# Requests on Pool spread out, and weight differences on VectorE placed behind PSUM copies, in an attention and maxout kernel

## The chip, the cores and the metric

The kernel runs on one core of a Trainium2 chip. The metric is the device time of one execution in microseconds. A core has five engines that matter here, each with its own instruction stream that it runs in order: PE (matrix multiply), DVE (VectorE), ACT (ScalarE), POOL (GpSimd, called Pool in the text) and SP (which only issues transfers). An engine that waits at one instruction runs nothing behind it.

## The reference, cut to what matters

Causal attention in blocks of 64 over 8 batches of 8 heads (576 positions, head size 64), and a maxout layer on its result:

```
scores = (q @ k^T) / 8, masked by blocks of 64;  a = softmax(scores);  x = a @ v
x      -> [4608 tokens, 512]
g      = maximum(x @ w1, x @ w2)            # 512 -> 1024
out    = g @ w_out                          # 1024 -> 512
```

The kernel rewrites the maxout. With D = w1 - w2, maximum(x w1, x w2) = x w2 + relu(x D). So

```
out = x @ M + relu(x @ D) @ w_out,   M = w2 @ w_out  (512 x 512, worked out once)
```

D is made by VectorE in four quarters of 256 columns, each as soon as that quarter of w1 has landed. M is made by TensorE in eight units: unit (i, c) is half i of the columns and row block c, and needs half i of w_out.

## The kernel before: the parts that matter

The program is a list of instructions that the author has put in order by hand (`manual_schedule`). The order of the calls below is, for each engine, the order in which that engine runs its share.

Loading and preparing. A "group" g is four heads, and has a request for q and one for k, 576 KB each. A request on SP is tied to Pool: a one-column memset of the target is put on Pool, and SP's request has to follow it. Requests of w1, w_out, w2 and v are issued by Pool itself.

```python
raw  = tile_pool(bufs=3)      wraw = tile_pool(bufs=4)
ps_s = PSUM pool, bufs=2 (scores)      ps_m = PSUM pool, bufs=4 (all else)

def load_qk(g, queues, gated=False):
    for nm, src, queue in (("q", q, queues[0]), ("k", k, queues[1])):
        if queue is None ...: continue
        raws[nm, g] = t = raw.tile([P, 2, RPP * D], FP32)
        if gated:
            nc.gpsimd.memset(t[:, 0, :1], 0.0)               # L114, Pool
        queue.dma_start(out=t[:], in_=...)                   # L115, SP

def cast(nm, g, parts):                  # fp32 -> bf16, on the engine that is named
    for copy, j0, j1 in parts:
        copy(out=n[:, j0:j1], in_=t[:, j0:j1])               # L155

def load_w1(j):                          # quarter j of w1, 512 KB
    nc.gpsimd.dma_start(out=w1_raw[j], in_=w1r[...])         # L177, Pool
def diff_w(j):                           # D of quarter j
    nc.vector.tensor_sub(d_sb[quarter j], w1_raw[j], w2_sb[j])   # L183, VectorE
def load_wo(i):                          # half i of w_out
    nc.gpsimd.dma_start(out=wo_sb[half i], in_=wor[...])     # L189, Pool
```

The units of TensorE that are put in wherever there is room. `fill(n)` emits the next ones: 8 matmuls of an M unit count 4, the 4 matmuls of an h unit count 4.

```python
def h_unit(i, f):      # 512 tokens i, 128 columns f of D; f = 2j, 2j+1 need diff_w(j)
    pt = ps_m.tile(...)
    for c in range(4):
        matmul(pt, d_sb[:, c, f], xT[:, c, tokens])          # L226
    nc.vector.tensor_scalar_max(g[:, f], pt, 0.0)            # L231, the relu

def m_unit(i, c):
    pt = ps_m.tile(...)
    for f in range(8):
        matmul(pt, bT_sb[:, f, c], wo_sb[:, f, half i])      # L249
    (act if i and c > 1 else dve)(out=m_sb[:, c, half i], in_=pt)    # L254

def transposes(nm, g, copies):           # two ps_m tiles; returns their copy-out
    for j in range(9):
        for i in range(2): nc.tensor.transpose(pts[i][:, j], n[...], ident)  # L357
    # copy_out: copies[i](out=qT or kT, in_=pts[i])                          # L365
```

The stage that is changed, as it was (cuts marked by dots):

```python
    av(2, [0, 1]); burst_q3(2); masks_q(2)
    load_qk(2, (SP, SP), gated=True)
    ...                                       # fills, bursts of scores, av
    burst_q3(3); masks_q(3)
    load_w1(0)
    load_qk(3, (SP, None), gated=True)        # q of group 3
    cast("q", 2, ((pool, 0, RPP),))
    load_qk(3, (None, SP), gated=True)        # k of group 3
    for j in range(1, d_ff // WB): load_w1(j)
    load_v(1, 0); load_v(1, 1)
    fill(8)                                   # M 0, 1
    av(3, [2, 3, 4])
    fill(4)                                   # M 2
    x_out(1, 0, NCH, (act, act))
    cast("k", 2, ((act, 0, RPP),))
    fill(4)                                   # M 3
    diff_w(0)
    fill(8)                                   # M 4, 5
    transposes("q", 2, (dve, act))()
    fill(4)                                   # M 6
    transposes("k", 2, (act, act))()
    pad_keys(4); pad_keys(5)
    diff_w(1)
    cast("q", 3, ((pool, 0, RPP),))
    load_v(1, 2); load_v(1, 3)
    load_qk(4, (SP, SP), gated=True)
    cast("k", 3, ((pool, 0, RPP),))
    load_v(1, 4)
    fill(4)                                   # M 7
    region(tile_0(4), tile_1(4), masked=False)
    fill(8)                                   # h 0, 1
    diff_w(2)
    region(tile_2(4), tile_0(5), masked=False)
    masks(4)
    fill(8)                                   # h 2, 3
    diff_w(3)
    copy_out = transposes("q", 3, (dve, act)) # ... h 4, transposes of k 3, and the main loop
```

Of the kernel before, what the change touches and what calls it, by code (L numbers as in the profile page):

```python
# [14 lines left out]
def kernel(  # L15
# [10 lines left out]
    nc = tc.nc  # L26
# [6 lines left out]
    d_model = H * D  # L33
    d_ff = moe_w1.shape[1]
    NDM = d_model // P
    NFF = d_ff // P
# [7 lines left out]
    RPP = S // NP  # L44
# [9 lines left out]
    NCH = 5  # L54
# [44 lines left out]
    wo_sb = wpool.tile([P, NFF, d_model], BF16, name="wo_sb")  # L99
# [5 lines left out]
    dve, pool, act = nc.vector.tensor_copy, nc.gpsimd.tensor_copy, nc.scalar.copy  # L105

    def load_qk(g, queues, gated=False):
        b, u = divmod(g, GPB)
        for nm, src, queue in (("q", q, queues[0]), ("k", k, queues[1])):
            if queue is None or by_dma(nm, g):  # L110
                continue
            raws[nm, g] = t = raw.tile([P, 2, RPP * D], FP32, name=f"{nm}raw")
            if gated:
                nc.gpsimd.memset(t[:, 0, :1], 0.0)  # L114
            queue.dma_start(  # L115
                out=t[:],
                in_=src[b, 4 * u:4 * u + 4].rearrange(
                    "(s h) (p t) d -> (h p) s (t d)", h=2, t=RPP),
            )
# [4 lines left out]
    def by_dma(nm, g):  # L124
        return g >= T_DMA.get(nm, NG)
# [21 lines left out]
    def cast(nm, g, parts):  # L147
        if by_dma(nm, g):
            return
        t = raws[nm, g].rearrange("p s (t d) -> p t s d", d=D)  # L150
        if (nm, g) not in qk_n:
            qk_n[nm, g] = qkn.tile([P, RPP, 2, D], BF16, name=f"{nm}n")
        n = qk_n[nm, g]
        for copy, j0, j1 in parts:
            copy(out=n[:, j0:j1], in_=t[:, j0:j1])  # L155
# [12 lines left out]
    WB = 256  # L168
# [6 lines left out]
    def load_w1(j):  # L175
        w1_raw[j] = wraw.tile([P, NDM, WB], FP32, name="w1raw")
        nc.gpsimd.dma_start(out=w1_raw[j][:], in_=w1r[:, :, j * WB:(j + 1) * WB])  # L177
# [4 lines left out]
    def diff_w(j):  # L182
        nc.vector.tensor_sub(d_sb[:, :, j * WB:(j + 1) * WB], w1_raw[j][:], w2_sb[j])  # L183
# [8 lines left out]
    dve, pool, act = nc.vector.tensor_copy, nc.gpsimd.tensor_copy, nc.scalar.copy  # L192
    SP, ACT = nc.sync, nc.scalar
    warm = small.tile([P, 1], FP32, name="warm")
# [132 lines left out]
    def fill(n):  # L327
        while n > 0:
            if not current:
                k = next((k for k, t in enumerate(todo) if t[2] <= done_tokens[0]), None)  # L330
                if k is None:
                    return max(0, n)
                current.append(todo.pop(k))
            t = current[0]
            next(t[1])
            n -= t[3]
            t[0] -= 1
            if not t[0]:
                current.pop()
        return 0  # L340
# [10 lines left out]
    def transposes(nm, g, copies):  # L351
        n = qk_n.pop((nm, g))
        pts = [ps_m.tile([P, RPP, NP], BF16, name=f"ps_{nm}T", tag="m") for _ in range(2)]
        for j in range(RPP):
            for i in range(2):
                r = slice(i * NP, (i + 1) * NP)
                nc.tensor.transpose(  # L357
                    pts[i][:, j, :], n[r, j].rearrange("p s d -> p (s d)"), ident[r, r],
                )

        def copy_out(which=(0, 1), part=(0, NP), copy=None):
            p0, p1 = part
            for i in which:
                t = (qT_r if nm == "q" else kT_r)[(2 * g + i) % NT]
                (copy or copies[i])(  # L365
                    out=t[:, p0 * RPP:p1 * RPP].rearrange("q (p j) -> q p j", j=RPP),
                    in_=pts[i][:, :, p0:p1].rearrange("q j p -> q p j"),
                )
        return copy_out

    def scores(p, ps, col, c, q0, w):
        qT, kT = qT_r[p % NT], kT_r[p % NT]
        k0 = min(c * P, S - P)
        for hh in range(2):
            r = slice(hh * D, (hh + 1) * D)
            nc.tensor.matmul(  # L376
                ps[:, hh, col:col + w], kT[r, k0:k0 + P], qT[r, q0:q0 + w],
                start=True, stop=True,
            )
# [9 lines left out]
    def corner_scores(p, ps, col):  # L389
        qT, kz = qT_r[p % NT], kz_r[p % NT]  # L390
        for k0, q0 in ((0, 384), (BLK, 512)):
            for hh in range(2):
                r = slice(hh * D, (hh + 1) * D)
                nc.tensor.matmul(  # L394
                    ps[:, hh, col:col + BLK], kz[r, k0:k0 + P], qT[r, q0:q0 + BLK],
                    start=(k0 == 0), stop=(k0 > 0),
                )

    def exp(p, ps, w, a0):
        nc.scalar.activation(  # L400
            out=aT_r[p % NA][:, :, a0:a0 + w], in_=ps[:, :, :w], func=AF.Exp, scale=scale,
        )

    def mask(p, a0, eng=None):
        (eng or nc.gpsimd).memset(aT_r[p % NA][BLK:, :, a0:a0 + BLK], 0.0)  # L405
# [20 lines left out]
    def burst_q3(p, warm=0):  # L426
        burst(p, ((3, 384, 192),), 1408, warm)
# [5 lines left out]
    def masks_q(p, eng=None):  # L433
        for a in (1024, 1408):
            mask(p, a, eng)
# [3 lines left out]
    def tile_0(p):  # L439
        u = ps_s.tile([P, 2, 512], FP32, name="ps_s", tag="s")  # L440
        scores(p, u, 0, 0, 0, 512)
        return lambda masked: (exp(p, u, 512, 0), masked and mask(p, 0))
# [7 lines left out]
    def tile_2(p):  # L450
        u = ps_s.tile([P, 2, 512], FP32, name="ps_s", tag="s")
        corner_scores(p, u, 320)
        scores(p, u, 0, 2, 256, 320)
        scores(p, u, 384, 3, 448, P)

        def out(masked):
            exp(p, u, 512, 1024)
            nc.scalar.activation(
                out=aT_r[p % NA][BLK:, :, 1536:AW], in_=u[BLK:, :, 320:320 + BLK],
                func=AF.Exp, scale=scale,  # L460
            )
            if masked:
                mask(p, 1024)
                mask(p, 1344)
        return out

    def masks(p):
        for a0 in (0, 576, 1024, 1344):
            mask(p, a0)

    def region(*tiles, masked=True):
        for out in tiles:
            out(masked)
# [29 lines left out]
    def x_by_dma(g):  # L503
        return BY_DMA <= g < NG - 1
# [10 lines left out]
    def x_out(g, t0=0, t1=NCH, copies=(dve, dve)):  # L515
        b, u = divmod(g, GPB)
        if x_by_dma(g):
            if u == GPB - 1:
                done_tokens[0] = (b + 1) * S
            return  # L520
        xp = xps[g]
        n = t1 - t0
        n_odd = min(t1, NCH - 1) - t0
        pe = ps_m.tile([P, 2, n, BLK], BF16, name="ps_xe", tag="m")
        po = ps_m.tile([P, 2, n_odd, BLK], BF16, name="ps_xo", tag="m")
        for s in range(2):
            for t in range(t0, t1):
                src = xp[:, s, t].rearrange("p a d -> p (a d)")
                nc.tensor.transpose(pe[:, s, t - t0, :], src[:BLK], ident[:BLK, :BLK])
                if t < NCH - 1:  # L530
                    nc.tensor.transpose(po[:, s, t - t0, :], src[BLK:], ident[BLK:, BLK:])
        dst = xT[:, 2 * u:2 * u + 2, b * S + t0 * P:b * S + t1 * P].rearrange(
            "p s (t h w) -> p s t h w", h=2, w=BLK)
        copies[0](out=dst[:, :, :, 0], in_=pe[:])
        copies[1](out=dst[:, :, :n_odd, 1], in_=po[:])
        if u == GPB - 1:
            done_tokens[0] = min(b * S + t1 * P, (b + 1) * S)
# [91 lines left out]
    av(2, [0, 1])  # L629
    burst_q3(2)  # L630
    masks_q(2)
    load_qk(2, (SP, SP), gated=True)
    fill(2)
    burst_q1(3)
    fill(2)
# [2 lines left out]
    av(2, [2, 3, 4])  # L638
    burst_q3(3)
    masks_q(3)  # L640
    load_w1(0)
    load_qk(3, (SP, None), gated=True)
    cast("q", 2, ((pool, 0, RPP),))
    load_qk(3, (None, SP), gated=True)
    for j in range(1, d_ff // WB):
        load_w1(j)
    load_v(1, 0)
    load_v(1, 1)
    fill(8)
    av(3, [2, 3, 4])  # L650
    fill(4)
    x_out(1, 0, NCH, (act, act))
    cast("k", 2, ((act, 0, RPP),))
    fill(4)
    diff_w(0)
    fill(8)
    transposes("q", 2, (dve, act))()
    fill(4)
    transposes("k", 2, (act, act))()
    pad_keys(4)  # L660
    pad_keys(5)
    diff_w(1)
    cast("q", 3, ((pool, 0, RPP),))
    load_v(1, 2)
    load_v(1, 3)
# [2 lines left out]
    load_v(1, 4)  # L668
    fill(4)
    region(tile_0(4), tile_1(4), masked=False)  # L670
    fill(8)
    diff_w(2)
    region(tile_2(4), tile_0(5), masked=False)
    masks(4)
    fill(8)
    diff_w(3)
    copy_out = transposes("q", 3, (dve, act))
    outs = tile_1(5), tile_2(5)
    copy_out()
# [96 lines left out]
```

## Time and profile before

| | before |
|---|---|
| median of 3 runs | 258.56 us (258.22 to 259.25) |
| span of the profiled execution | 256.4 us |
| PE busy | 241.1 us (94%) |
| DVE busy | 150.6 us (59%) |
| ACT busy | 120.6 us (47%) |
| POOL busy | 121.0 us (47%) |
| granted TensorE clock | 0.998 |

The page gives busy times over the whole span. A view of windows gives, for each stretch of time, the busy microseconds of each engine with the number of instructions in brackets. A timeline gives start, duration, engine and source line of each instruction, and in square brackets how long the engine had been idle before it and who released it. The list of waits adds these idle times up by pair, as total, count and longest. The chain is followed back from the last instruction, at each step to what released it. A transfer's time "to landing" runs from the start of its issue.

### The profile page before, as it was taken

To read this page: it belongs to the slowest core of one execution; us is meant where nothing else is said; L and a number is where in the kernel's file an instruction comes from. 1 tells how busy PE (TensorE), PEld (TensorE's weight loads), DVE (VectorE), ACT (ScalarE), POOL (GpSimd) and SP (SyncE) were. 2 spreads that over 40 slices of the span, in tenths; PEclk is the share of its full clock that TensorE was granted. 3 is DMA by queue.
4 is the path that set the end of the run, shared out by engine and by line. 5 is a ranking of instruction groups with operands and counts; after the bars stand their busy time and mean duration, and the time that the engine had idled before them with its cause. 6 is when DMAs were issued, how large, how long until landed. Compare 5 with 4: busy or idle time off the path is not lost.

```text
span 256.4 us, 6716 instructions
## 1 busy us (share of the span) xinstructions
PE 241.1 (94%) x2732; PEld 133.2 (52%) x2768; DVE 150.6 (59%) x301; ACT 120.6 (47%) x159; POOL 121.0 (47%) x288
## 2 busy tenths in 40 slices
PE   8798887998999999999999999999999999999994
PEld 2466743565555555555555555455545564444443
DVE  4987469657485457545753575357635754753521
ACT  2876378657774655646464646464646300000000
POOL 1972673669769466955675577547231100000000
PEclk9999999999999999999999999999999999999999
DMA  7999999779999999999999999999961312111122
GB/s 243 216 159 226 348 326 205 221 60 217 158 177 190 163 239 153 233 166 223 145 209 161 220 146 205 158 218 166 108 139 58 81 43 82 42 42 42 73 90 83
DMA packets 104383, 41.27 MB, mean 161 GB/s; under 512 B 89248, under 2 KB 93728, under 8 KB 104352
## 3 DMA queue, kind: packets, MB, share of 16 engines
q0 software_dynamic: 65952, 11.87, 60.4%
q1 hardware_dynamic: 37984, 28.32, 48.7%
q10 hardware_dynamic: 416, 0.66, 0.7%
q8 instruction: 21, 0.34, 0.6%
q14 instruction: 10, 0.08, 0.1%
HBM read 34.60 MB, written 9.44 MB: 172 GB/s over the span
## 4 chain that ended last, share of the span: by engine, by line
PE 85%; DMA 5%; DVE 4%; issue 3%; ACT 2%; POOL 0%; POOLq 0%
PE ps_y L268 35%; PE ps_h L226 23%; PE ps_o L491 11%; PE ps_s L376 8%; DMA w1raw<-in_moe_w_dram 3%; DMA qraw<-in_q_dram 2%; PE ps_w L346 2%; PE ps_qT L357 2%; DVE d_sb L183 2%; ACT aT L400 2%; DVE g L231 1%; PE ps_y L283 1%; PE ps_s L394 1%; PE ps_s L411 1%; PE ps_bT L238 0%
## 5 line engine op out<-in xcount | busy, mean ns | idle before, releaser
L400 ACT ACTIVATE aT<-ps_s 128x1024 bf16<-128x1024 f32 (+2 forms) x100 | 95.8, 994 | 45.4 <-PE ps_s L376 33.9
L226 PE MATMUL ps_h<-xT,d_sb 128*128 128x512 bf16 x277 | 67.1, 379 | 2.7 <-DVE qT L365 1.0
L268 PE MATMUL ps_y<-wo_sb,g 128*128 128x512 bf16 x261 | 66.7, 379 | 2.6 <-issue 2.5
L231 DVE TENSOR_SCALAR g<-ps_h 128x512 bf16<-128x512 f32 x72 | 49.4, 689 | 16.4 <-PE ps_h L226 16.4
L405 POOL MEMSET aT<- 64x128 bf16 x128 | 22.8, 200 | 65.6 <-ACT aT L400 64.7
L273 DVE COPY y<-ps_y 128x512 f32<-128x512 f32 x35 | 24.2, 691 | 46.2 <-PE ps_y L268 45.6
L491 PEld LDWEIGHTS <-aT 128*128 128x128 bf16 x960 | 37.4, 98 | 14.0 <-issue 0.7
L226 PEld LDWEIGHTS <-d_sb 128*128 128x128 bf16 x288 | 26.5, 98 | 32.8 <-issue 4.1
L268 PEld LDWEIGHTS <-g 128*128 128x128 bf16 x280 | 24.8, 98 | 30.2 <-issue 5.5
L491 PE MATMUL ps_o<-vv,aT 128*128 128x65 bf16 x960 | 39.8, 194 | 0.0
L268 PE MATMUL ps_y<-m_sb,xT 128*128 128x512 bf16 x136 | 37.2, 379 | 0.4 <-issue 0.2
L159 POOL DMA_DIRECT2D vv<-in_v_dram x40 | 34.1, 859 | 0.9 <-issue 0.5
L376 PE MATMUL ps_s<-qT,kT 64*128 64x128 bf16 (+6 forms) x344 | 31.4, 281 | 1.6 <-ACT kT L365 0.7
L498 DVE TENSOR_TENSOR xp<-ps_o,rec 128x256 bf16<-128x256 f32 (+1 forms) x64 | 31.4, 491 | 2.2
L132 POOL DMA_DIRECT2D kb<-in_k_dram x40 | 29.4, 761 | 0.0
L497 DVE RECIPROCAL rec<-ps_o 128x4 f32<-128x4 f32 (+1 forms) x64 | 12.0, 187 | 24.1 <-PE ps_o L491 23.4
L288 ACT COPY y<-ps_y 128x256 f32<-128x256 f32 (+1 forms) x2 | 0.6, 319 | 49.3 <-PE ps_y L283 49.3
L365 ACT COPY qT<-ps_qT 128x576 bf16<-128x576 bf16 x15 | 9.6, 639 | 23.3 <-PE ps_qT L357 21.8
L155 POOL CAST qn<-qraw 128x1152 bf16<-128x1152 f32 (+1 forms) x15 | 16.5, 1100 | 7.6 <-DMA qraw<-in_q_dram 7.6
L268 PEld LDWEIGHTS <-xT 128*128 128x128 bf16 x140 | 12.8, 98 | 14.0 <-issue 0.7
L376 PEld LDWEIGHTS <-kT 64*128 64x128 bf16 x344 | 11.8, 94 | 12.4 <-issue 7.1
L365 DVE COPY qT<-ps_qT 128x576 bf16<-128x576 bf16 x17 | 12.7, 749 | 0.5 <-PE ps_qT L357 0.5
(58 smaller groups left out, 137.3 us busy)
## 6 DMA issues: line engine op xcount, KB each, us to landing
qraw<-in_q_dram SPq DMA_DIRECT2D x16, 576.0 KB, 5.0
out_dram<-y SPq DMA_DIRECT2D x35, 256.0 KB, 4.1
vv<-in_v_dram POOLq DMA_DIRECT2D x32, 128.0 KB, 5.8
kraw<-in_k_dram SPq DMA_DIRECT2D x5, 576.0 KB, 7.6
kb<-in_k_dram POOLq DMA_DIRECT2D x40, 72.0 KB, 6.8
w1raw<-in_moe_w_dram POOLq DMA_DIRECT2D x4, 512.0 KB, 7.1
xT<-in_moe_w_dram POOLq DMA_DIRECT2D x4, 256.0 KB, 6.5
wo_sb<-in_moe_w_out_dram POOLq DMA_DIRECT2D x2, 512.0 KB, 10.3
```

Of the source, the lines that this page charges most:

```text
L132: nc.gpsimd.dma_start(out=n[h * BLK:(h + 1) * BLK, :, s], in_=(q if nm == "q" else k)[b, 4 * u + 2 * s + h].rearrange("(j p) d -> p j d", ...
L159: nc.gpsimd.dma_start(out=vv_r[b % NV][P - rows:, c, :, :D], in_=v[b, :, c * P:c * P + rows, :].rearrange("h p d -> p h d"),)
L226: nc.tensor.matmul(pt[:], d_sb[:, c, f * P:(f + 1) * P], xT[:, c, t0:t0 + SPAN], start=(c == 0), stop=(c == NDM - 1),)
L231: nc.vector.tensor_scalar_max(g[:, f], pt[:], 0.0)
L268: nc.tensor.matmul(py[:], lhs, rhs, start=(n == 0), stop=(n == len(terms) - 1),)
L273: nc.vector.tensor_copy(out=y[:], in_=py[:])
L365: (copy or copies[i])(out=t[:, p0 * RPP:p1 * RPP].rearrange("q (p j) -> q p j", j=RPP), in_=pts[i][:, :, p0:p1].rearrange("q j p -> q p j"),)
L376: nc.tensor.matmul(ps[:, hh, col:col + w], kT[r, k0:k0 + P], qT[r, q0:q0 + w], start=True, stop=True,)
L400: nc.scalar.activation(out=aT_r[p % NA][:, :, a0:a0 + w], in_=ps[:, :, :w], func=AF.Exp, scale=scale,)
L405: (eng or nc.gpsimd).memset(aT_r[p % NA][BLK:, :, a0:a0 + BLK], 0.0)
L491: nc.tensor.matmul(po[:, gi, hh, :], a[:, hh, a0:a0 + P], vv[:, c, h0 + 2 * hh, :], start=(mm == 0), stop=(mm == n_mm - 1),)
L498: nc.vector.tensor_mul(xp[:, :, ts[0]:ts[0] + n, p % 2].rearrange("q s t d -> q t s d"), po[:, :, :, :D], rec[:, :n].to_broadcast([P, n, 2 ...
```

## The change: what it does and what it is for

Requests first. The requests of q and k of group 2 went out together; now k's goes out later, behind the masks of pair 3. The request of w1's second quarter, which stood behind the cast of q of group 2, now stands before it, and behind a new one-column copy on Pool that reads the second half of w_out, so that Pool gets there only when w_out has landed. The requests of q and k of group 3 are moved behind the cast and mixed with those of the last two quarters of w1. The aim is that requests reach the DMA engines in the order in which they are needed, rather than in a bunch.

VectorE second. The difference of a quarter of w1 waits for a transfer, and while it waits nothing behind it on VectorE runs. The first two differences are moved behind the PSUM copies of six units of M and the copy of qT, and the last two are put in behind a single h unit each instead of behind two. One of the copies of x moves from ACT to VectorE, and ACT's cast of k of group 2 moves behind its copy of qT.

```diff
-    load_qk(2, (SP, SP), gated=True)
+    load_qk(2, (SP, None), gated=True)
 ...
     masks_q(3)
+    load_qk(2, (None, SP), gated=True)
     load_w1(0)
+    nc.gpsimd.tensor_copy(out=warm[:], in_=wo_sb[:, NFF - 1, d_model - 1:])
+    load_w1(1)
+    cast("q", 2, ((pool, 0, RPP),))
     load_qk(3, (SP, None), gated=True)
-    cast("q", 2, ((pool, 0, RPP),))
+    load_w1(2)
+    load_w1(3)
     load_qk(3, (None, SP), gated=True)
-    for j in range(1, d_ff // WB):
-        load_w1(j)
 ...
-    x_out(1, 0, NCH, (act, act))
+    x_out(1, 0, NCH, (act, dve))
+    fill(4)
+    transposes("q", 2, (dve, act))()
     cast("k", 2, ((act, 0, RPP),))
-    fill(4)
+    fill(8)
     diff_w(0)
-    fill(8)
-    transposes("q", 2, (dve, act))()
+    diff_w(1)
     fill(4)
     transposes("k", 2, (act, act))()
     pad_keys(4)
     pad_keys(5)
-    diff_w(1)
 ...
     region(tile_0(4), tile_1(4), masked=False)
-    fill(8)
+    fill(4)
     diff_w(2)
+    fill(4)
     region(tile_2(4), tile_0(5), masked=False)
     masks(4)
-    fill(8)
+    fill(4)
     diff_w(3)
+    fill(4)
     copy_out = transposes("q", 3, (dve, act))
```

The fills add up to the same number of units before and after, so that from the transposes of q of group 3 on the program is the same.

## The prediction, on record before the changed kernel was seen

> **What bounds the kernel now.** I read the shares of the page first (PE 241.1 us of 256.4, so TensorE is the bound over the whole), then cut the span into windows to see where TensorE is not busy. Columns: window, its length, then busy time and instruction count of PE, PE's weight loads, DVE, ACT and POOL.
>
> ```profile
> 23.00:46.00 23.00, 18.49 (x243) 11.79 (x242) 15.83 (x24) 13.48 (x21) 12.97 (x28) 1.00 1.29 286
> 46.00:100.00 54.00, 52.09 (x736) 30.34 (x746) 32.88 (x72) 35.05 (x46) 39.00 (x91) 1.00 1.37 175
> 100.00:200.00 100.00, 97.94 (x1113) 53.24 (x1126) 57.02 (x118) 54.01 (x70) 55.84 (x134) 1.00 1.40 170
> ```
>
> From 46 us on TensorE idles 1.9 us in 54 and 2.1 us in 100. In the changed stage, 23 to 46 us, it idles 23.00 - 18.49 = 4.5 us. That is the most the change can bring, since it removes no matmul. TensorE's own waits in that stage say what it stood for:
>
> ```profile
> PE ps_M L249 <- DVE m_sb L254: 1.5, 1, 1.5
> PE ps_h L226 <- DVE qT L365: 1.0, 1, 1.0
> PE ps_M L249 <- DMA wo_sb<-in_moe_w_out_dram: 0.9, 1, 0.9
> PE ps_h L226 <- DVE g L231: 0.7, 1, 0.7
> PE ps_s L376 <- DVE kT L365: 0.2, 1, 0.2
> ```
>
> Four of the five name VectorE: PSUM tiles that it was late to copy out. 1.5 + 1.0 + 0.7 + 0.2 = 3.4 us. Why was it late? Its timeline, first the M stage, then the h stage:
>
> ```profile
> 31.15 1.23 DVE L183 TENSOR_TENSOR d_sb<-w1raw,xT 128x1024 bf16<-128x1024 f32 x1 [1.55 <-DMA w1raw<-in_moe_w_dram]
> 32.29 0.75 DVE L254 CAST m_sb<-ps_M 128x256 bf16<-128x256 f32 x2
> ...
> 35.72 2.18 DVE L183 TENSOR_TENSOR d_sb<-w1raw,xT 128x1024 bf16<-128x1024 f32 x1 [2.01 <-DMA w1raw<-in_moe_w_dram]
> 37.82 1.28 DVE L231 TENSOR_SCALAR g<-ps_h 128x512 bf16<-128x512 f32 x2
> 39.02 1.82 DVE L183 TENSOR_TENSOR d_sb<-w1raw,xT 128x1024 bf16<-128x1024 f32 x1
> ```
>
> The first difference stood on VectorE waiting for w1's first quarter until 31.15, and two finished M tiles stood behind it until 32.29: that is TensorE's 1.5 us. The second waited for the second quarter until 35.72, and from there VectorE was busy without a break to 45.7. The chain of waits goes the same way (start, us, what):
>
> ```profile
> 21.63 6.37 DMA qraw<-in_q_dram
> ...
> 28.15 1.06 issue
> ...
> 29.25 6.45 DMA w1raw<-in_moe_w_dram
> 35.70 0.02 issue
> 35.72 1.87 DVE d_sb L183
> 37.59 0.23 issue
> 37.82 1.28 DVE g L231 x2
> ```
>
> It reads: q of group 2 lands at 28.0; only then can Pool cast it (the 1.06 us shown as issue) and pass on to the request of w1's second quarter at 29.25; that lands 6.45 us later and starts VectorE's long run, which ends with the copy of kT of group 3 at 45.1, when TensorE can go on.
>
> **What the Trainium skill says.** Three places bear on it.
> - "DMA: Bandwidth & Descriptors", the section on the anatomy of one DMA, gives about 2.0 us fixed plus bytes / 436 GB/s; an estimate from that page for a 512 KB quarter is 2.0 + 1.2 = 3.2 us. The trace shows 6.4 to 8.1 us for the four, so they share the DMA engines. The section on queues and rings of the same page says that each engine takes turns between the rows that have work. The trace agrees in kind: from 26 to 28 us SP's row moved 0.64 MB and Pool's 0.18 MB at once. It also says that DMA engines don't wait on semaphores, the issuing engine does; this is how the new copy on Pool can hold a request back.
> - "SBUF — State Buffer", "Who interferes with whom": a VectorE instruction with two SBUF inputs contends with a GpSimd instruction that reads SBUF, and the later one is blocked. The trace agrees: the differences at 35.72 and 39.02 took 2.18 and 1.82 us, beside Pool's casts of q and k at 35.67 (1.15 us) and 38.57 (1.18 us), those at 31.15 and 41.95 beside no cast took 1.23 and 1.21.
>
> **The change part by part.**
>
> 1. *Request of k, group 2, later* (22.0 to about 24.2, right after the masks of pair 3 that end at 24.1). Transfers of SP's queue began moving only at about 24.4 and q takes them till 28.0, so k is behind q either way. It landed at 22.04 + 8.9 = 30.9; I expect 30.9 to 31.3. Worth 0.
>
> 2. *Copy on Pool that waits for w_out.* The second half of w_out was asked for at 16.55 and took 10.9 us: 27.45. Pool gets to the copy at about 25, so it stands idle until 27.5, which it did anyway (it waited 3.05 us for q until 28.13). Then w1's second quarter goes out at about 27.6 instead of 29.25: 1.6 us earlier. Its issue costs 0.75 us, so that the cast of q starts at about 28.35 instead of 28.13 and ends at 29.5.
>
> 3. *Second quarter of w1.* With the same 6.45 us it lands at 34.1 instead of 35.7. It may gain a little more: q of group 3 is asked for at about 29.6 instead of 25.1, and between 30 and 32 us Pool's row moved only 0.02 MB while SP's moved 0.49, which this request can now use. I take 34.0. The third and fourth quarters are issued at about 29.8 and 30.5 (before 30.0 and 30.7) and are behind the same bytes; 37.2 and 38.8 before, I take 36.5 and 38.2. q and k of group 3 (before 32.7 and 34.2) come to about 34.3 and 36.5; they are needed by casts at about 34.6 and 37.6, so nearly nothing is lost.
>
> 4. *Differences behind the M copies.* TensorE runs M 3 till 29.0, then the transposes of q of group 2, which must wait for the cast that ends at 29.5: a new wait of 0.5 us. Then M 4 and 5 to 31.7, M 6 to 32.6, with VectorE free to copy: the 1.5 us wait goes. ACT casts k when it has landed, 31.1 to 32.2, so k's transposes can follow M 6 without a gap. ACT then copies M 6 (0.4) and two kT (0.6 each), so scores of pair 4 start at about 33.9 instead of 35.07, and the first exponential at about 34.7 instead of 35.57. About 1.0 us is gained by here.
>
> 5. *VectorE's run.* The second difference goes 34.0 to 35.2, or to 35.8 if Pool's cast of q of group 3 (from about 34.6) comes beside it. Then relu of h 0 (0.64, since two take 1.28), third difference from 36.5 or when VectorE is free, 1.2 to 1.8: to 38.0. Two relus to 39.3, fourth difference to 40.6, then relu 0.64, qT 0.68, relu 0.64, kT 0.68: 40.6 + 2.6 = 43.2, where the chain of before has the copy of kT end at 45.1. That is 1.9 us earlier.
>
> 6. *ACT.* From the first exponential to the last kT copy it needed 35.57 to 43.8, some 8.2 us, nearly full. Starting at 34.7 it ends at 42.9 at the latest. It is no tighter than VectorE.
>
> 7. *Copy of x moved to VectorE*: 0.59 us off ACT, where there was 1.7 us of waiting for k behind it, and 0.4 us onto VectorE at about 28.8, where it idled. Worth 0.
>
> By the other way of counting, what idle time of TensorE is left between 23 and 46 us: 0.9 for w_out's first half stays, 0.5 before the transposes of q is new, the 1.5 of M 6 goes, and of the 1.9 around h and the last kT (1.0 + 0.7 + 0.2) I leave 1.4, as VectorE is still nearly full there. That is 2.8 of 4.5 us, a gain of 1.7. The two counts say 1.9 and 1.7; I take 1.8. After 46 us TensorE is 96 to 98% busy and the instructions are the same, so what is gained is kept. 258.56 - 1.8 = 256.8.
>
> **The rivals.**
> - *The DMA engines are the bound.* From 24 to 38 us they move 250 to 410 GB/s, and the same bytes must come: w1's quarters would land hardly earlier, whatever the order of requests. For it: SP's row and Pool's row share. Against it: 254 GB/s from 30 to 32 us beside 411 from 26 to 28, so there is room. It would leave the gain of part 4 alone, about 1.0: 257.6.
> - *Pool becomes the bound.* The copy blocks the cast of q, and the later requests of group 3 are late, so that the transposes of q and k of group 3 wait. If w_out lands a microsecond later than before, everything on Pool follows. Against it: Pool idled 3.05 us there already, and the casts of group 3 have about 0.3 and 1 us to spare. It would cost 1 to 2 us in place of the gain: 257 to 259.
> - *All VectorE waits go.* All 3.4 us come back if the third and fourth quarters also land 1.5 to 2 us earlier: 255.2. Against it: their requests are not earlier, and ACT's 8.2 us of work stands close behind.
>
> **Range and chances.** 256.8, with 255.5 for the third rival nearly whole, and 258.3 for the first or second together with the spread of before (258.22 to 259.25). Two per cent faster would be 253.4, more than all 4.5 us of idle TensorE: 0.02. Two per cent slower needs 5.2 us of new waits, which only a late group 3 or something I don't see could make: 0.02.
>
> **What would show it.** Right: the wait of M on VectorE's m_sb gone; w1's second quarter issued at 27.5 to 27.8 and landed at 33.5 to 34.5; first exponential of pair 4 at 34.5 to 35; kT of group 3 copied at 43 to 43.6; windows from 46 us on the same but for a shift of 1.5 to 2 us. Wrong: Pool past 28 at its copy; second quarter after 35; the third difference idle for more than 1 us with two h tiles standing behind it; TensorE waiting for casts of group 3; or a gain at 45 us that is lost between 46 and 60 to later loads of group 4.

## The result and the profile after

| | before | changed |
|---|---|---|
| median | 258.90 us (258.22 to 259.31, 4 runs) | 262.28 us (261.31 to 262.79, 4 runs) |
| span of the profiled execution | 256.4 us | 260.9 us |
| granted TensorE clock of it | 0.998 | 0.986 |

The ratio is 1.0129, with a 95% interval of 1.0088 to 1.0170. The change made the kernel slower by 1.3%, where a gain of 0.7% was predicted (256.8 us, with a range of 255.5 to 258.3).

The same three windows as shown for the kernel before (length, then busy time and count of PE, weight loads, DVE, ACT, POOL; then the granted clock, DMA share and GB/s):

```profile
23.00:46.00 23.00, 21.28 (x296) 13.85 (x296) 17.78 (x31) 15.95 (x23) 15.75 (x35) 1.00 1.10 253
46.00:100.00 54.00, 48.99 (x680) 28.21 (x689) 29.36 (x65) 31.41 (x42) 36.09 (x81) 0.97 1.27 172
100.00:200.00 100.00, 98.05 (x1111) 53.23 (x1125) 57.13 (x117) 54.90 (x71) 57.87 (x137) 1.00 1.51 176
```

The stage that was changed did get denser: TensorE idles 1.7 us of 23 instead of 4.5. The loss lies in the second row, where TensorE idles 5.0 us instead of 1.9 and the clock column reads 0.97. A finer cut of the second row in the changed kernel shows where the clock is low:

```profile
52.00:54.00 2.00, 1.67 (x11) 0.66 (x7) 1.07 (x2) 1.88 (x4) 0.65 (x4) 0.59 0.18 62
54.00:56.00 2.00, 2.00 (x12) 1.02 (x11) 0.51 (x2) 0.98 (x1) 0.55 (x3) 0.56 0.00 0
```

TensorE counts as busy here, at 0.59 and 0.56 of its clock: 2 x 0.41 + 2 x 0.44 = 1.7 us of work lost. TensorE's waits in the changed stage, and then the first line of its waits from 46 us to the end, both of the changed kernel (total, count and longest in us; L357 are the transposes of q and k, L491 is the product with v):

```profile
PE ps_kT L357 <- POOL kn L155: 1.2, 1, 1.2
PE ps_qT L357 <- POOL qn L155: 0.2, 1, 0.2
PE ps_h L226 <- issue: 0.2, 1, 0.2
```

```profile
PE ps_o L491 <- DMA vv<-in_v_dram: 3.0, 2, 2.1
```

Nothing waits for VectorE any more. In its place TensorE waits for Pool's cast of k of group 3, and for 3.0 us for v of batch 1, on which it never waited before. The chain of the changed kernel between 29 and 52 us says how v came to be late (start, us, what):

```profile
29.98 8.32 DMA qraw<-in_q_dram
...
38.45 0.91 POOL qn L155
39.36 0.83 issue
40.19 1.55 POOL vv L159 x2
...
43.27 7.93 DMA vv<-in_v_dram
51.20 0.04 issue
51.24 0.34 PE ps_o L491 x6
```

q of group 3 is asked for at 29.98 and lands 8.32 us later. Pool stands at its cast until then, and the requests of v stand behind that cast: the last goes out at 43.27, where before it went out at 39.65, and needs 7.9 us to land in both. It lands at 51.2 instead of 47.6.

The changed kernel's shift against the one before, step by step: VectorE's copy of kT of group 3 ends at 44.6 instead of 45.1; the transposes of q of group 4 start at 51.51 instead of 48.65; those of k of group 4 at 57.03 instead of 52.53; the end is at 260.9 instead of 256.4. So: 0.5 ahead, then 2.9 behind (3.4 us, 3.0 of it the wait for v), then 4.5 behind (1.6 us for the clock), and no more after that. This execution had also started the stage late: M's first unit ran at 25.94 instead of 24.21, because a quarter of w2, asked for ahead of anything that was changed, landed at 18.0. TensorE waited 1.1 us for it, and the clock was then 0.55 from 18 to 20 us and 0.59 from 20 to 22. So the mean clock of 0.986 has two low stretches in it, and only the one from 52 us on comes after the changed stage. The late start isn't the change's, as the repeat below shows.

### The profile page after: what moved, and what is told of

Read it like the earlier page. It is cut to its first block, busy times and chain, and to the rows that moved or that the text cites. A ratio compares the mean times of both kernels' runs of the same rounds, so it can differ in the third digit from the quotient of the medians.

```text
span 260.9 us, 6715 instructions
## 1 busy us (share of the span) xinstructions
PE 243.7 (93%) x2732; PEld 134.8 (52%) x2768; DVE 150.0 (57%) x302; ACT 120.1 (46%) x158; POOL 122.9 (47%) x289
## 4 chain that ended last, share of the span: by engine, by line
PE 79%; DMA 11%; POOL 4%; issue 3%; ACT 1%; DVE 0%; POOLq 0%
PE ps_y L268 35%; PE ps_h L226 21%; PE ps_o L491 10%; PE ps_s L376 8%; DMA qraw<-in_q_dram 5%; DMA vv<-in_v_dram 3%; DMA xT<-in_moe_w_dram 3%; POOL vv L159 2%; PE ps_qT L357 2%; PE ps_y L283 1%; ACT aT L400 1%; PE ps_bT L238 1%; POOL qn L155 1%; PE ps_s L394 1%; POOL w1raw L177 1%
## 5 line engine op out<-in xcount | busy, mean ns | idle before, releaser
L268 PE MATMUL ps_y<-wo_sb,g 128*128 128x512 bf16 x261 | 67.6, 383 | 2.6 <-issue 2.5
L273 DVE COPY y<-ps_y 128x512 f32<-128x512 f32 x35 | 24.2, 691 | 46.2 <-PE ps_y L268 45.6
L491 PEld LDWEIGHTS <-aT 128*128 128x128 bf16 x960 | 38.5, 99 | 17.7 <-issue 4.6
L491 PE MATMUL ps_o<-vv,aT 128*128 128x65 bf16 x960 | 41.1, 195 | 3.0 <-DMA vv<-in_v_dram 3.0
L497 DVE RECIPROCAL rec<-ps_o 128x4 f32<-128x4 f32 (+1 forms) x64 | 12.0, 187 | 29.9 <-PE ps_o L491 29.4
L365 ACT COPY qT<-ps_qT 128x576 bf16<-128x576 bf16 x15 | 9.6, 640 | 27.6 <-PE ps_qT L357 26.2
L155 POOL CAST qn<-qraw 128x1152 bf16<-128x1152 f32 (+1 forms) x15 | 17.2, 1145 | 8.4 <-DMA qraw<-in_q_dram 8.3
```

The source lines that it names most:

```text
L268: nc.tensor.matmul(py[:], lhs, rhs, start=(n == 0), stop=(n == len(terms) - 1),)
L273: nc.vector.tensor_copy(out=y[:], in_=py[:])
L365: (copy or copies[i])(out=t[:, p0 * RPP:p1 * RPP].rearrange("q (p j) -> q p j", j=RPP), in_=pts[i][:, :, p0:p1].rearrange("q j p -> q p j"),)
L491: nc.tensor.matmul(po[:, gi, hh, :], a[:, hh, a0:a0 + P], vv[:, c, h0 + 2 * hh, :], start=(mm == 0), stop=(mm == n_mm - 1),)
```

## The experiments

The theory: requests that go out later make q of group 3 late; Pool, waiting for it, asks for v late; TensorE waits for v; and its clock drops after the wait. Rivals: the later q and k themselves, the new copy on Pool, the new places of VectorE's differences, chance in the first result, or full DMA engines. The ratios leave out executions more than 1.5% above the fastest of the same kernel, all of these with a mean clock below 0.995; counts of executions below are of all. For scale, before was 258.7 to 258.8 us beside these kernels. An execution's mean clock says that the clock was low for a while, and not where.

### The change in its two halves

Requests alone (VectorE's and ACT's order as before) and VectorE's and ACT's order alone (requests as before):

```diff
 # requests alone, on the kernel before
-    load_qk(2, (SP, SP), gated=True)
+    load_qk(2, (SP, None), gated=True)
 ...
-    load_w1(0); load_qk(3, (SP, None)); cast("q", 2); load_qk(3, (None, SP)); load_w1(1..3)
+    load_qk(2, (None, SP)); load_w1(0); copy of w_out; load_w1(1); cast("q", 2)
+    load_qk(3, (SP, None)); load_w1(2); load_w1(3); load_qk(3, (None, SP))
```

> The kernel before with the changed order of requests on Pool alone; VectorE's differences and ACT's copies stay as before. Theory (the requests made the loss): v is again late, 260.5 to 264. Rival (the loss needs VectorE's earlier work, which makes TensorE come to v sooner): 258 to 259.5, as before.

> The kernel before with the changed places of VectorE's differences and ACT's copies alone; all requests as before. Theory: q of group 3 lands at about 32.7, v is asked for at 36 to 40 as before, and TensorE comes to v up to 2 us sooner, so a part of the gain is spent on a wait for v of 0 to 1.5 us: 257 to 259. Rival (the differences' new places are what costs): 260 to 263.

Requests alone: ratio 1.0005 (0.9984 to 1.0027), the same time. TensorE waits 1.7 us for v and still 1.7 us for VectorE's M copies. The time of 260.5 to 264 that the theory gave was wrong; the rival's was right: requests alone make v late, but TensorE is late as well.

VectorE's order alone: ratio 0.9956 (0.9940 to 0.9972), 1.1 us faster, as expected. TensorE's waits from 23 to 46 us in it begin so:

```profile
PE ps_h L226 <- DVE d_sb L183: 1.3, 1, 1.3
PE ps_M L249 <- DMA wo_sb<-in_moe_w_out_dram: 0.9, 1, 0.9
```

The wait of M on VectorE is gone, and of v there is none. The second difference waits for its quarter of w1 until 36.22, since that quarter is asked for as late as before. None of its 20 executions has a mean clock below 0.995, where before has 30 of 71 beside it. The other 41 of before have a median of 258.31 us, so that by this estimate about 0.4 of the 1.1 us goes with the clock. Where before's clock is low wasn't traced.

The halves don't add up: -0.4% and +0.05% alone, +0.9 to +1.3% together. In the profiles TensorE came to the 24 products with v at 47.83 us before, 47.92 with VectorE's order alone, 47.12 with the requests alone, and 45.36 in the repeat of both below. The last request of v went out at 39.65, 39.20, 43.00 and 41.20. So the requests bring v later, and it takes both halves to bring TensorE to v much sooner: the earlier quarter of w1, and a VectorE that is free to use it.

### The changed kernel again

> The changed kernel once more, beside the other three on one chip. Theory (q of group 3 lands at about 38, v is asked for behind it, TensorE waits about 2 to 3 us for v and in most executions its clock then drops): 260 to 262.5 in the median, most executions below a clock of 0.995, v waited for 1.5 us or more. Rival (the first result was one chip's or one run's chance, above all the late start before 23 us): 257.5 to 259, as the part kernels gave.

Ratio 1.0091 (1.0061 to 1.0120), 2.4 us slower (1.1% by the medians of all executions, 261.61 and 258.68 us), so the first result was no chance. This execution wasn't late at the start (M's first unit at 23.93, before 24.21), and its waits from 24 us on are:

```profile
PE ps_o L491 <- DMA vv<-in_v_dram: 4.1, 2, 2.4
PE ps_kT L357 <- POOL kn L155: 1.0, 1, 1.0
```

Coming to v earlier, TensorE waits longer for it. kT of group 3 is copied at 42.57 at the latest, 2.5 us ahead of before; the transposes of q of group 4 start at 50.73, 2.1 behind; those of k of group 4 at 55.91, 3.4 behind; the end is 3.2 behind. The clock is 0.58 and 0.57 from 50 to 54 us. So the gain was there, 2.5 us, and was lost to about 4.6 us at v (4.1 of it the wait) and 1.3 at the low clock. 15 of its 17 executions have a mean clock below 0.995; of VectorE's order alone, none of 20.

### v ahead of the cast, and q of group 3 earlier

Two ways to break the chain at different links: the requests of v no longer behind the cast of q of group 3, or q of group 3 asked for where it was.

```diff
 # v first
+    load_v(1, 2); load_v(1, 3); load_v(1, 4)
     cast("q", 3, ((pool, 0, RPP),))
-    load_v(1, 2); load_v(1, 3)
     load_qk(4, (SP, SP), gated=True)
     cast("k", 3, ((pool, 0, RPP),))
-    load_v(1, 4)
```

```diff
 # q of group 3 early
     load_w1(0)
+    load_qk(3, (SP, None), gated=True)
     nc.gpsimd.tensor_copy(out=warm[:], in_=wo_sb[...])
     load_w1(1)
     cast("q", 2, ((pool, 0, RPP),))
-    load_qk(3, (SP, None), gated=True)
```

> The changed kernel with the three late requests of v of batch 1 put ahead of Pool's cast of q of group 3. Theory (the loss is v: Pool waits for q of group 3, v is asked for behind it, TensorE waits for v and its clock drops): v is asked for 3 to 5 us earlier than 40.2 to 43.3, TensorE's 3.0 us wait for v goes, the granted clock from 52 to 56 us is 1.0, and the time is 256.5 to 258. Rival (the loss is the later q and k of group 3 themselves, or the later start of the M units): 260 to 262, with a wait on casts of group 3 in place of v.

> The changed kernel with only the request of q of group 3 put back to where it stood, behind the first quarter of w1. Theory (q of group 3 lands 8.3 us after a request at 30.0 and holds up v): it is asked for at about 28 or earlier and lands at 33 to 36, Pool's cast no longer waits, v is asked for 2 to 3 us earlier, 257 to 259. Rival (q lands late because the DMA engines are full, whenever it is asked for): lands at 37 to 38, 261 to 263.

v first: ratio 0.9979 (0.9953 to 1.0005), 2.9 us below the repeat of the changed kernel by the ratios (1.0091 - 0.9979 = 1.1%). v is asked for from 35.45 on, and TensorE doesn't wait for it. It waits for casts instead, 1.3 us at q of group 4 and 0.5 at k of group 3 among them: the rival had a part.

q early: ratio 0.9951 (0.9930 to 0.9972). q of group 3 is asked for at 25.4 and lands at 33.0, 7.6 us later. Its landing takes 6.4 to 8.6 us in the kernels here, whenever it is asked for, so the rival of full DMA engines falls: a later request is a later landing. A wait for v of 1.9 us is left in the profile: v's last part is still asked for only at 42.09, since Pool's cast of k of group 3 ahead of it waited 1.5 us for TensorE's transposes of q.

### The last request of v ahead of group 4

```diff
     load_v(1, 2); load_v(1, 3)
+    load_v(1, 4)
     load_qk(4, (SP, SP), gated=True)
     cast("k", 3, ((pool, 0, RPP),))
-    load_v(1, 4)
```

> The changed kernel with only the last request of v put ahead of the requests of q and k of group 4 and of the cast of k of group 3; q of group 3 stays late. Theory (v's small packets are held up by q and k of group 4, which SP's row moves beside them): the last part of v lands 6 to 7 us after its request and 2 us or more sooner than in the changed kernel, TensorE waits for v at most 1.5 us, 258.3 to 260. Rival (q of group 3 alone is the cause): v lands only the 1.2 us of the cast sooner, and the wait stays at 2 us or more, 260 to 261.5.

258.05 us, a little less than was expected, and a ratio of 0.9968 (0.9948 to 0.9988). Moving this one request ahead of two requests and a cast was worth 1.2% by the two ratios (1.0091 and 0.9968). No wait for v is left. Pool's timeline in this kernel, and TensorE's at the product with v:

```profile
37.37 1.15 POOL L155 CAST qn<-qraw 128x1152 bf16<-128x1152 f32 x1 [1.12 <-DMA qraw<-in_q_dram]
38.45 2.44 POOL L159 DMA_DIRECT2D vv<-in_v_dram  x3
```

```profile
47.17 0.89 PE L491 MATMUL ps_o<-vv,aT 128*128 128x65 bf16 x24
```

q of group 3 still comes late (Pool is still released by it at 37.4), yet the 24 products run in one piece (TensorE then waits 0.85 us for the cast of q of group 4 instead). The last part of v lands 6.0 us after its request at 40.2, in place of 7.9 and 9.1 in the two profiles of the changed kernel. Why it took longer there is in the DMA view by queue (packets, MB, share of 16 engines; q0 is Pool's row, q1 SP's). The changed kernel from 42 to 44 us, and then from 44 to 46, when q of group 4, asked for at 42.1, begins to move:

```profile
q0 software_dynamic: 1311, 0.17, 135.4%
...
q1 hardware_dynamic: 214, 0.48, 79.4%
q0 software_dynamic: 372, 0.05, 36.5%
```

With the engines nearly to itself v moved 0.17 MB in 2 us, in 1311 packets of some 130 bytes; beside q of group 4 it moved 0.05 in 372, while q had 214 packets of some 2.2 KB. The Trainium skill, "DMA: Bandwidth & Descriptors", queues and rings, says that an engine takes turns between rows by the packet. Packet counts of one order and bytes that differ tenfold agree with it in kind: the row of small packets loses. (The page's packet is made up of several descriptors; whether the profile counts the same unit isn't shown.) v's last part stood behind the rest of v in that row.

### Idle matmuls where TensorE waits

```diff
         av(p, [0, 1])
         fill(n)
+        if p == 4:
+            warm_up(9)             # nine 128x512 matmuls on zeros
         av(p, [2, 3, 4])
```

> The changed kernel with nine idle matmuls of 128x512 on zeros (about 1.95 us at 0.216 us each) put before the product that waits for v; their result isn't used. Theory (idle TensorE lowers its clock, and that costs a further 1 to 1.7 us behind the wait): the wait for v shrinks to about 1 us, the clock from 52 to 56 us is 1.0, time 0.8 to 1.7 us below the changed kernel. Rival (the clock is low for another reason, or the drop costs nothing): time as the changed kernel, or up to 1 us above it where v isn't late.

Ratio 1.0043 (1.0020 to 1.0066), so 0.5% or 1.2 us below the repeat beside it on the same chip (the two intervals just touch), though TensorE has 2 us more to do. 6 of its 20 executions have a clock below 0.995, where the repeat had 15 of 17. What was expected of a profile with v late:

> The changed kernel with nine idle matmuls ahead of the product that waits for v, for a profile. Theory: TensorE is busy while v comes, a wait for v of about 1 to 2 us is left, and the clock is 1.0 from 46 to 60 us. Rival: the clock falls to about 0.57 for some 4 us all the same.

TensorE's timeline of it:

```profile
45.87 2.11 PE L346 MATMUL ps_w<-zeros 128*128 128x512 bf16 x8
47.81 0.71 PE L491 MATMUL ps_o<-vv,aT 128*128 128x65 bf16 x18
49.60 0.34 PE L491 MATMUL ps_o<-vv,aT 128*128 128x65 bf16 x6 [1.08 <-DMA vv<-in_v_dram]
```

The first wait is filled, 1.08 us of the second is left, and the clock is 1.00 in every window of 2 us from 46 to 60.

### Without the copy that waits for w_out

```diff
-    nc.gpsimd.tensor_copy(out=warm[:], in_=wo_sb[:, NFF - 1, d_model - 1:])
```

> The changed kernel without the copy on Pool that waits for w_out. Theory (the copy is minor: q of group 3 is still asked for behind the cast of q of group 2): w1's second quarter is asked for at about 25, the cast of q of group 2 moves from 28.5 to about 28.1, q of group 3 is asked for at 29.3, v stays late; time 0 to 1 us below the changed kernel. Rival (the copy is what makes Pool late): 2 us or more below it, with no wait for v.

Ratio 1.0015 (0.9989 to 1.0041), 0.8% or 2.0 us below the repeat: more than the 1 us that I allowed. v is late all the same (2.3 us of waiting in its profile), and 10 of its 20 executions have a low clock instead of 15 of 17.

The copy ties Pool's order to a landing that varies: it ran at 26.6 to 28.7 us in the profiles above, and at 31.04 in one execution with idle matmuls (263.82 us), where the second half of w_out took 14.5 us to land. The cast of q of group 2 began there at 32.02, and TensorE stood at that group's transposes:

```profile
33.23 0.44 PE L357 MATMUL ps_qT<-ident,qn 64*128 64x64 bf16 x18 [3.24 <-POOL qraw L114]
```

After it the clock was 0.66 from 34 to 36 us and 0.50 from 36 to 38, and TensorE didn't wait for v. Elsewhere, with VectorE's new order, the same wait was 0.7 us where the cast began at 28.3 (without the copy) and 1.6 us where it began at 29.6. So the copy has a second way to cost time, at q of group 2, which has nothing to do with v. How the 2.0 us divide between this and a shorter wait for v isn't shown.

### The parts joined

q of group 3 early, no copy, v's last request ahead of group 4:

```diff
     load_w1(0)
-    nc.gpsimd.tensor_copy(out=warm[:], in_=wo_sb[...])
+    load_qk(3, (SP, None), gated=True)
     load_w1(1)
     cast("q", 2, ((pool, 0, RPP),))
-    load_qk(3, (SP, None), gated=True)
 ...
     load_v(1, 3)
+    load_v(1, 4)
     load_qk(4, (SP, SP), gated=True)
     cast("k", 3, ((pool, 0, RPP),))
-    load_v(1, 4)
```

> The changed kernel with q of group 3 asked for ahead of w1's second quarter, no copy, and the last request of v ahead of the requests of group 4 and the cast of k of group 3. Theory (Pool's order is the cause of all that was lost): no wait for v above 0.5 us, cast of q of group 2 at about 28.3, second difference before 35.5, clock 1.0, time 254.8 to 256.6, faster than both kernels. Rival (the transfers are the bound and one wait takes the place of another): 257 to 258.5, as the first four part kernels.

257.00 us, ratio 0.9935 (0.9913 to 0.9956): faster than both kernels, by 1.7 us against before, but short of the 254.8 to 256.6 that I expected, and at the edge of the rival's 257 to 258.5. Its waits from 24 to 64 us:

```profile
PE ps_qT L357 <- POOL qn L155: 1.6, 2, 1.0
PE ps_kT L357 <- POOL kn L155: 0.4, 1, 0.4
PE ps_kT L357 <- DVE y L273: 0.4, 1, 0.4
```

v is gone from the list, and of VectorE only 0.4 us at y (L273) is left, which the kernel before has too. What is left is mostly Pool's casts of q: 0.6 us at group 2, and 1.0 us at group 4, whose transfer lands at 46.2. That is the rival's account: one wait has taken the place of another.

## Why the prediction was wrong, by its own steps

- **Parts 1 and 2 (k later, the copy)** held in their times or came sooner: in the profile that started on time k of group 2 landed at 29.4 (30.9 predicted), the copy ran at 26.59 and the second quarter of w1 was asked for at 26.82 (27.6 predicted). That the copy costs nothing didn't hold: without it the changed kernel was 2.0 us faster, and the second rival's "if w_out lands a microsecond later than before, everything on Pool follows" was seen in a trace.
- **Part 4 (differences behind the M copies)** held. VectorE's order alone removed the 1.5 us wait of M. The new wait that it foresaw at q of group 2, 0.5 us, ran from nothing to 3.2 us in the profiles. With the stage on time, the changed kernel even reached the end of kT at 42.57, where part 5 said 43.2.
- **Part 5 (VectorE's run)** held in kind. VectorE's timeline of the changed kernel, the counterpart of the one shown for before:

```profile
34.91 1.23 DVE L183 TENSOR_TENSOR d_sb<-w1raw,xT 128x1024 bf16<-128x1024 f32 x1 [0.17 <-DMA w1raw<-in_moe_w_dram]
36.86 0.69 DVE L231 TENSOR_SCALAR g<-ps_h 128x512 bf16<-128x512 f32 x1 [0.72 <-PE ps_h L226]
38.00 1.23 DVE L183 TENSOR_TENSOR d_sb<-w1raw,xT 128x1024 bf16<-128x1024 f32 x1 [0.46 <-DMA w1raw<-in_moe_w_dram]
```

  The second difference starts at 34.91 instead of 35.72, takes 1.23 instead of 2.18, and no finished M tile stands behind it. This time Pool was the one held up: its cast of q of group 3 began at 38.45, during the third difference, and took 1.79 us where its others took 1.15. That agrees with the Trainium skill, "SBUF — State Buffer", "Who interferes with whom", by which the later of the two is blocked.
- **Part 3 is the step that failed.** It put q of group 3 at "about 34.3" and said that "nearly nothing is lost". q landed at 38.3 (37.0 in the repeat). I worked from the landing of before plus a share for the gap, instead of from the time from request to landing, which the profile had: 29.6 + 7.6 is 37.2.
- **The part that was missing: v.** I listed casts as what needs q of group 3, and not the requests of v that stand on Pool behind that cast. Nor did I ask when v is needed. In the kernel before, v's last part was asked for at 39.65 and took 7.9 us: it landed at 47.6. The 24 products with v started at 47.83, and the six that need the last part come last, at about 48.4 (an estimate from the 0.89 us that the 24 took). So there was some 0.8 us of slack, less than the 1.8 us of gain predicted, and a gain beyond it had to turn into a wait unless v came sooner too. The prediction's list of what would show it wrong had "a gain at 45 us that is lost between 46 and 60", but laid it to loads of group 4.
- **"What is gained is kept", since TensorE is 96 to 98% busy after 46 us**, failed for the same reason: a busy engine shows no wait for a transfer that lands just in time. From 46 to 100 us TensorE idled 5.0 us instead of 1.9.
- **The clock** was in no step. After the wait of 3 to 4 us it cost another 1.3 to 1.7 us.
- **The rivals.** "Pool becomes the bound" was the nearest, and was set aside on the ground that Pool had idled 3.05 us there already; it named late requests of group 3 as the cause, but the transposes of that group as what would wait, and not v. Full DMA engines weren't the cause, though how two rows share them set how late v came.

## What to carry to other kernels

Before moving a request, list every request that stands behind the same wait on the issuing engine, and set each one's landing against the first use of its data; a gain on one side of a just-in-time transfer becomes a wait on the other. Changes that are harmless alone can cost together: here one put the producer back, and the two together brought the consumer forward. Ask for the small and slow transfers ahead of the large ones that will share the DMA engines with them.

## What the runs showed of the hardware that was not expected

- After waits for v of 3.0 and 4.1 us, each in two pieces, the granted clock of TensorE fell to half for some 3 us (0.50 in windows of half a microsecond from 52.5 to 55.5 us in the changed kernel, and from 50.5 to 53.5 in its repeat). Idle matmuls in the wait kept it at 1.00. The Trainium skill, "TensorE: Matmul & The Clock Gate", Part 1, has this: after an idle window of about 3.4 us the clock falls to half, and the window runs freely, so that the point varies. The half agrees. The length doesn't come out of these runs as a limit: 2.3 us in two pieces lowered the clock (0.54 and 0.60 from 50 to 54 us, without the copy), and so did a single wait of 1.1 us for w2 (0.50 from 18.5 to 21.5 us, changed kernel), while single waits of 1.7 and 1.9 us for v left it alone in two profiles. No wait length that is safe is shown.
- How far the row of small packets gives way to one of large packets: 0.05 MB in 2 us beside it, 0.17 without.
